# Batch 0's queries in token order by the copy out of PSUM, and corner zeros behind the next pair's copy: a blockwise-causal attention with a gated FFN on one core

## The chip, the cores and the metric

The kernel runs on one NeuronCore of one Trainium2 chip. The metric is the time of one execution on the device, in microseconds. The engines are named as in the profile: PE is the tensor engine's matmuls and PEld its weight loads, DVE the vector engine, ACT the scalar engine, POOL is GpSimd, and SP the engine that issues most of the DMAs. Each engine works through its own instructions in program order.

## The reference

Queries, keys and values are float32 of shape (8 batches, 8 heads, 576 tokens, 64). The attention is causal by blocks of 64 tokens: a query sees all keys of its own block and of the blocks before it. The attention's output, with the heads side by side, is 4608 rows of 512, and goes through a gated FFN of width 1536.

```python
scores = (1 / np.sqrt(D)) * np.matmul(q, k.transpose(0, 1, 3, 2))
mask = (pos[:, None] // 64) >= (pos[None, :] // 64)
scores = np.where(mask, scores, -1e9)
attn = softmax(scores)
x = np.matmul(attn, v).transpose(0, 2, 1, 3).reshape(4608, 512)
out = (np.maximum(x @ w_gate, 0.0) * (x @ w_val)) @ w_out
```

## The kernel before

**Tiles.** The first 512 tokens of a batch are four chunks of 128 (`c`), the last 64 are the tail. Heads go in pairs: a pair's two heads lie on partitions 0 to 63 and 64 to 127. A block of work `r` is a batch and a pair, `r = 4 * b + hp`. The tiles `qTm` and `kTm` hold a batch's queries and keys transposed, [128 partitions, 4, 4 pairs, 128]; there are two of each, used in turn by the batches.

**How queries and keys get there.** Batches 0 and 1 are loaded by `Early.load_qk` so that a partition holds four neighbouring tokens (token = 4 * p + j): that makes the DMA's pieces long. `cast_qk` makes bfloat16 of them. `pe_mains` (L351) then transposes a pair on PE, first four matmuls for the queries and then four for the keys, each into a bank of PSUM; the columns come out with `j` outermost. Two copies, `evac[0]` for the queries and `evac[1]` for the keys, take them to SBUF. The key copy (L365) reads PSUM with `j` inside, so `kTm` is in token order. For batch 0 alone, the query copy (L363) keeps `j` outermost, and `qTm` of batch 0 is [partition, j, pair, p].

**Scores.** `scores` (L464) makes scores transposed: keys are the stationary operand, queries the moving one, one matmul for each chunk of keys and each head of the pair. For chunk `c` it takes queries from chunk `c` on, so 512, 384, 256 or 128 columns. The function `queries` (L457) gives the moving operand. For batch 0 it puts the tokens in order in the read itself: for each `m`, the four `j` that are 512 elements apart. For the other batches the read goes along memory within a chunk.

```python
if b == 0:
    return m[ps, :, hp, 32 * c : 128].rearrange("p j m -> p m j")
return m[ps, c:4, hp, :]
```

`scores_of(g)` (L481, batch 0) does a third of a block: chunk 0, chunks 1 and 3, or chunk 2, into one of two pairs of score banks in turn, and ACT takes the exponential (L479) of both heads at once. `scores_all` does a whole block for the later batches. `corners` and `corner` (L536 to L544) zero the 64 x 64 corners of the diagonal chunks that the mask forbids, after the exponentials. `head_av` (L591) multiplies by the values (L605), with a column of ones that gives the sum; `normalise` (L549) divides by it; `to_xT_pe` (L645) transposes the result for the FFN.

**FFN.** `ffn_gen` (L684) is a generator: for a batch, 12 groups of gate and value matmuls (L700), ReLU on ACT (L709), the product on DVE (L714), then the output matmuls (L729). `ffn(n)` emits at least `n` matmuls of it; `ffn_parts(n)` emits `n` parts of four matmuls.

**Order.** All engines' orders are written out by hand (`manual_schedule`, from L788). Batch 0 comes first: for its four pairs, `pe_mains` with the copies on (DVE, ACT) for pair 0 and (DVE, DVE) for the other three, between calls of `scores_of` 0 to 11. Then value matmuls and transposes, with 12 FFN matmuls between them, and then the FFN of batch 0 in full. POOL does the casts of queries, keys, values and weights, and most of batch 0's corners. SP's queue loads, in order, batch 0's queries, keys and values, the FFN weights by halves, batch 1, and the tails. PSUM has eight banks; 6 and 7 (`AV`) are used by the value matmuls, by `pe_mains` of batch 1, and by `sort_v` (L300), which puts batch 1's values in token order by matmuls (L308).

Block 4 (the first of batch 1) is reached inside the FFN of batch 0. Its order is the second place that the change touches:

```python
e1.pe_mains(0, (dve, act), banks[:, AV : AV + 2])
ffn(8)
scores_all(4, False)
corners(4, nc.vector)
e1.pe_mains(1, (dve, act), banks[:, AV : AV + 2])
ffn(8)
e1.sort_v(0, (dve, act), banks[:, AV : AV + 2])
```

Of the kernel before, what the change touches and what calls it, by code (L numbers as in the profile page):

```python
# [17 lines left out]
def kernel(  # L18
# [29 lines left out]
    banks = psum.tile([128, 8, 512], FP, name="banks")  # L48
    AV = 6
# [8 lines left out]
    def pair():  # L58
        return take(2)

    def as_bf(bank):
        return bank.bitcast(BF)
# [8 lines left out]
    qTm = [consts.tile([128, 4, 4, 128], BF, name=f"qTm{i}") for i in range(2)]  # L71
    kTm = [consts.tile([128, 4, 4, 128], BF, name=f"kTm{i}") for i in range(2)]
    qTt = [consts.tile([128, 4, 64], BF, name=f"qTt{i}") for i in range(2)]
# [113 lines left out]
    class Early:  # L187
# [163 lines left out]
        def pe_mains(self, hp, evac, out=None):  # L351
            out = out or pair()
            for t in range(2):
                tp = as_bf(out[:, t, :])[:, 0:512]
                src = self.half(t, hp // 2)
                lo = 128 * (hp % 2)
                for j in range(4):
                    nc.tensor.transpose(  # L358
                        tp[:, 128 * j : 128 * j + 128], src[:, j, lo : lo + 128], ident
                    )  # L360
                dst = (qTm, kTm)[t][self.b % 2][:, :, hp, :]
                if self.b == 0 and t == 0:
                    evac[t](dst, tp.rearrange("p (j m) -> p j m", j=4))  # L363
                else:
                    evac[t](  # L365
                        dst.rearrange("p c (n j) -> p c n j", j=4),
                        tp.rearrange("p (j c n) -> p c n j", j=4, c=4),
                    )

        def pe_tails(self, evac):  # L370

# [82 lines left out]
            eng(dst, st)  # L454


    def queries(b, ps, c, hp):  # L457

        m = qTm[b % 2]
        if b == 0:  # L460
            return m[ps, :, hp, 32 * c : 128].rearrange("p j m -> p m j")
        return m[ps, c:4, hp, :]

    def scores(b, hp, sc, pieces):  # L464
        for pos, c, main in pieces:
            for hh in range(2):
                ps = slice(64 * hh, 64 * hh + 64)
                n = 512 - 128 * c if main else 64
                x = queries(b, ps, c, hp) if main else qTt[b % 2][ps, hp, :]
                o = sc[:, hh, pos : pos + n]  # L470
                if main:
                    o = o.rearrange("p (m n) -> p m n", n=4 if b == 0 else 128)
                nc.tensor.matmul(  # L473
                    o, kTm[b % 2][ps, c, hp, :], x, start=True, stop=True
                )
        return sc

    def exp(out, sc):
        nc.scalar.activation(out, sc, AF.Exp, scale=scale)  # L479

    def scores_of(g):  # L481

        r, i = divmod(g, 3)
        pieces = [[(0, 0, True)], [(0, 1, True), (384, 3, True)], [(0, 2, True)]][i]
        lo, hi = [(0, 512), (512, 1024), (1024, 1280)][i]
        sc = scores(0, r, banks[:, 0:2] if g % 2 == 0 else banks[:, 2:4], pieces)
        exp(attn(r, lo, hi), sc[:, :, 0 : hi - lo])

    def scores_all(r, tails=True):

        b, hp = divmod(r, 4)
        at = attnT[r % 2]
        sc = [
            scores(b, hp, pair(), [(0, 0, True)]),
            scores(b, hp, pair(), [(0, 1, True), (384, 3, True)]),
            scores(
                b, hp, pair(),
                [(0, 2, True)]
                + [(256 + 64 * c, c, False) for c in range(4 if tails else 0)],
            ),  # L500
        ]
        for hh in range(2):
            exp(at[:, hh, 0:512], sc[0][:, hh, :])
        exp(at[:, :, 512:1024], sc[1])
        w = 512 if tails else 256
        exp(at[:, :, 1024 : 1024 + w], sc[2][:, :, 0:w])
# [29 lines left out]
    def corners(r, eng):  # L536

        at = attnT[r % 2]
        three = at[64:128, :, 0:1536].rearrange("p g (c n) -> p g c n", c=3)
        eng.memset(three[:, :, :, 0:64], 0.0)  # L540
        eng.memset(at[64:128, :, 896:960], 0.0)
# [213 lines left out]
    def ffn(n):  # L755

        done[0] += n
        while part[0] < done[0]:
            ended = False
            while not ended:  # L760
                ended = next(gen, None)
                if ended is None:
                    return
                part[0] += 4
# [22 lines left out]
    dve, act, pool = nc.vector.tensor_copy, nc.scalar.copy, nc.gpsimd.tensor_copy  # L787
    with tc.manual_schedule(engines={E.PE, E.DVE, E.Activation, E.Pool, E.SP}):  # L788
# [64 lines left out]
        e1 = Early(1)  # L853
# [21 lines left out]
        e1.pe_mains(0, (dve, act), banks[:, AV : AV + 2])  # L875
        ffn(8)
        scores_all(4, False)
        corners(4, nc.vector)
        e1.pe_mains(1, (dve, act), banks[:, AV : AV + 2])
        ffn(8)  # L880
        e1.sort_v(0, (dve, act), banks[:, AV : AV + 2])
        ffn(8)
# [53 lines left out]
        for r in range(8, 4 * B):  # L936
            b, hp = divmod(r, 4)
# [78 lines left out]
```

## Time and profile before

| | |
|---|---|
| median of 3 runs | 378.8 us |
| lowest and highest run | 377.69 and 378.98 us |
| the profiled execution | 378.14 us |
| its span | 376.3 us |
| mean granted clock of the tensor engine | 0.982 |

The profile shows one execution. Times in it count from the start of the span. A group of instructions is a line, an engine, an operation and its tiles, with its count, its busy time, the mean of one in nanoseconds, and, behind the bar, the engine's idle time just ahead of them and what ended it. The chain of waits goes back from the last instruction, at each step to what released it. Tile names in batch 0's exponentials (`attnT`, `v_p`, `wo`) are buffers that lend their space.

### The profile page before, as it was taken

To read this page: it belongs to the slowest core of one execution; us is meant where nothing else is said; L and a number is where in the kernel's file an instruction comes from. 1 tells how busy PE (TensorE), PEld (TensorE's weight loads), DVE (VectorE), ACT (ScalarE), POOL (GpSimd) and SP (SyncE) were. 2 spreads that over 40 slices of the span, in tenths; PEclk is the share of its full clock that TensorE was granted. 3 is DMA by queue.
4 is the path that set the end of the run, shared out by engine and by line. 5 is a ranking of instruction groups with operands and counts; after the bars stand their busy time and mean duration, and the time that the engine had idled before them with its cause. 6 is when DMAs were issued, how large, how long until landed. Compare 5 with 4: busy or idle time off the path is not lost.

```text
span 376.3 us, 7510 instructions
## 1 busy us (share of the span) xinstructions
PE 367.1 (98%) x2993; PEld 189.5 (50%) x2993; DVE 164.7 (44%) x329; ACT 171.6 (46%) x269; POOL 116.0 (31%) x161
## 2 busy tenths in 40 slices
PE   7999989999999999999999999999999999999995
PEld 2354445555555555555555455545555554444443
DVE  4434345356655654354434443444344434323432
ACT  4644554755856654365436543654355503302310
POOL 5586764656908600950095005000000000000000
PEclk9669999999999999999999999999999999999999
DMA  8999999989999973996299639154301130020003
GB/s 251 292 371 358 371 210 308 169 206 253 158 108 134 128 136 66 133 166 131 62 154 152 109 85 141 42 102 92 99 17 17 44 101 1 3 84 28 2 34 106
DMA packets 139891, 51.02 MB, mean 136 GB/s; under 512 B 119504, under 2 KB 133072, under 8 KB 139856
## 3 DMA queue, kind: packets, MB, share of 16 engines
q1 hardware_dynamic: 78448, 34.29, 40.4%
q0 software_dynamic: 56704, 8.13, 37.1%
q10 hardware_dynamic: 4704, 8.13, 6.0%
q8 instruction: 23, 0.38, 0.4%
q14 instruction: 12, 0.10, 0.1%
HBM read 37.75 MB, written 9.44 MB: 125 GB/s over the span
## 4 chain that ended last, share of the span: by engine, by line
PE 96%; ACT 1%; DVE 1%; issue 0%; POOL 0%; DVEq 0%; ACTq 0%; POOLq 0%
PE banks L700 50%; PE banks L729 25%; PE banks L605 8%; PE banks L473 8%; PE banks L358 1%; PE banks L650 1%; PE banks L777 1%; PE banks L572 1%; PE banks L308 1%; ACT attnT L479 0%; DVE hT L714 0%; DVE ob L741 0%; ACT v_p L479 0%; ACT kTt L384 0%; PE banks L512 0%
## 5 line engine op out<-in xcount | busy, mean ns | idle before, releaser
L479 ACT ACTIVATE attnT<-banks 128x1024 bf16<-128x1024 f32 (+1 forms) x118 | 85.1, 805 | 63.4 <-PE banks L473 63.4
L709 ACT ACTIVATE gate_sb<-banks 128x512 bf16<-128x512 f32 x108 | 65.0, 603 | 101.4 <-PE banks L700 101.1
L714 DVE TENSOR_TENSOR hT<-gate_sb,banks 128x512 bf16<-128x512 bf16 x108 | 74.0, 688 | 78.8 <-PE banks L700 75.0
L700 PE MATMUL banks<-xT,wg 128*128 128x512 bf16 x384 | 99.8, 382 | 1.2 <-DVE xT L655 0.8
L700 PE MATMUL banks<-xT,wv 128*128 128x512 bf16 x384 | 98.5, 379 | 0.0
L729 PE MATMUL banks<-wo,hT 128*128 128x512 bf16 (+1 forms) x444 | 97.0, 373 | 0.0
L700 PEld LDWEIGHTS <-wv 128*128 128x128 bf16 x432 | 42.3, 98 | 51.0
L729 PEld LDWEIGHTS <-hT 128*128 128x128 bf16 x444 | 42.4, 98 | 46.1
L700 PEld LDWEIGHTS <-wg 128*128 128x128 bf16 x432 | 40.6, 98 | 46.2 <-issue 2.3
L741 DVE COPY ob<-banks 128x512 f32<-128x512 f32 (+1 forms) x37 | 25.1, 677 | 56.0 <-PE banks L729 55.9
L408 POOL DMA_DIRECT2D v_bf<-in_v_dram x16 | 14.3, 910 | 78.9 <-PE banks L605 78.9
L605 PEld LDWEIGHTS <-attnT 128*128 128x128 bf16 x792 | 29.9, 99 | 11.1 <-issue 3.3
L605 PE MATMUL banks<-v_bf,attnT 128*128 128x65 bf16 x792 | 34.5, 196 | 0.0
L473 PE MATMUL banks<-qTm,kTm 64*128 64x512 bf16 (+3 forms) x256 | 31.6, 349 | 1.3 <-DVE hT L714 0.4
L554 DVE TENSOR_TENSOR xnat<-banks,recip 128x640 bf16<-128x640 f32 (+2 forms) x36 | 25.9, 721 | 1.4 <-DVE recip L553 0.2
L553 DVE RECIPROCAL recip<-banks 128x10 f32<-128x10 f32 (+3 forms) x38 | 8.0, 210 | 35.7 <-PE banks L605 34.1
L473 PEld LDWEIGHTS <-kTm 64*128 64x128 bf16 x512 | 16.5, 95 | 12.3 <-issue 3.1
L540 DVE MEMSET attnT<- 64x192 uint32 x28 | 6.1, 218 | 22.0 <-ACT attnT L479 19.1
L408 POOL DMA_DIRECT2D k_bf<-in_k_dram x16 | 14.1, 911 | 1.4 <-DMA v_bf<-in_v_dram 1.4
L408 POOL DMA_DIRECT2D q_bf<-in_q_dram x16 | 14.3, 937 | 0.5 <-DMA v_bf<-in_v_dram 0.5
L700 PE MATMUL banks<-xTt,wg 128*128 128x512 bf16 x48 | 12.3, 379 | 0.0
L700 PE MATMUL banks<-xTt,wv 128*128 128x512 bf16 x48 | 12.3, 379 | 0.0
(101 smaller groups left out, 207.7 us busy)
## 6 DMA issues: line engine op xcount, KB each, us to landing
out_dram<-ob ACTq DMA_DIRECT2D x28, 256.0 KB, 2.2
stage<-in_moe_w_gate_dram SPq DMA_DIRECT2D x6, 512.0 KB, 9.3
stage<-in_moe_w_val_dram SPq DMA_DIRECT2D x6, 512.0 KB, 9.4
stage<-in_q_dram SPq DMA_DIRECT2D x6, 512.0 KB, 6.4
stage<-in_k_dram SPq DMA_DIRECT2D x6, 512.0 KB, 7.6
stage<-in_moe_w_out_dram SPq DMA_DIRECT2D x6, 512.0 KB, 9.7
stage<-in_v_dram SPq DMA_DIRECT2D x8, 256.0 KB, 6.3
q_bf<-in_q_dram POOLq DMA_DIRECT2D x16, 128.0 KB, 6.0
```

The costliest lines, as they stand in the source:

```text
L408: nc.gpsimd.dma_start(dst, src[b, :, 128 * c : 128 * c + n, :].rearrange("h p d -> p h d"),)
L473: nc.tensor.matmul(o, kTm[b % 2][ps, c, hp, :], x, start=True, stop=True)
L479: nc.scalar.activation(out, sc, AF.Exp, scale=scale)
L540: eng.memset(three[:, :, :, 0:64], 0.0)
L553: nc.vector.reciprocal(recip, av[:, :, :, 64])
L554: nc.vector.tensor_tensor(out=out, in0=av[:, :, :, 0:64], in1=recip.to_broadcast([rows, heads, n, 64]), op=AX.mult,)
L605: nc.tensor.matmul(av[:, 0, p, :], w, vb[:, c, h, :], start=(p == 0), stop=(c == p), skip_group_check=True,)
L700: nc.tensor.matmul(out[f][:, t, :], (wg, wv)[t][i][:, c, fo : fo + 128], x[:, c, :], start=(c == 0), stop=(c == 3),)
L709: nc.scalar.activation(gate[f], out[f][:, 0, :], AF.Relu)
L714: nc.vector.tensor_tensor(out=h, in0=gate[f], in1=out[f][:, 1, :], op=AX.mult)
L729: nc.tensor.matmul(ops[:, g, 0 : n1 - n0], hT[f][:, 128 * s : 128 * (s + 1)], wo[i][:, f % 4, n0:n1], start=(f == 0), stop=(f == 11),)
L741: nc.vector.tensor_copy(ob, ops[:, g, 0 : n1 - n0])
```

## The change

The query copy of batch 0 takes the form of the key copy: it reads PSUM with `j` inside and writes `qTm` along memory in token order. The function `queries` goes; the scores of batch 0 read their moving operand as those of the other batches do, and the view of the output follows. The number of matmuls, copies and columns is the same.

Besides, `corners(4)` on DVE is put behind `e1.pe_mains(1)`, whose query copy is on DVE too. The two swap places in DVE's order; no other engine's order changes.

```diff
@@ -358,14 +358,12 @@ (pe_mains)
-                dst = (qTm, kTm)[t][self.b % 2][:, :, hp, :]
-                if self.b == 0 and t == 0:
-                    evac[t](dst, tp.rearrange("p (j m) -> p j m", j=4))
-                else:
-                    evac[t](
-                        dst.rearrange("p c (n j) -> p c n j", j=4),
-                        tp.rearrange("p (j c n) -> p c n j", j=4, c=4),
-                    )
+                evac[t](
+                    (qTm, kTm)[t][self.b % 2][:, :, hp, :].rearrange(
+                        "p c (n j) -> p c n j", j=4
+                    ),
+                    tp.rearrange("p (j c n) -> p c n j", j=4, c=4),
+                )
@@ -454,22 +452,15 @@
-    def queries(b, ps, c, hp):
-
-        m = qTm[b % 2]
-        if b == 0:
-            return m[ps, :, hp, 32 * c : 128].rearrange("p j m -> p m j")
-        return m[ps, c:4, hp, :]
-
     def scores(b, hp, sc, pieces):
...
-                x = queries(b, ps, c, hp) if main else qTt[b % 2][ps, hp, :]
+                x = qTm[b % 2][ps, c:4, hp, :] if main else qTt[b % 2][ps, hp, :]
                 o = sc[:, hh, pos : pos + n]
                 if main:
-                    o = o.rearrange("p (m n) -> p m n", n=4 if b == 0 else 128)
+                    o = o.rearrange("p (c n) -> p c n", n=128)
@@ -875,8 +866,8 @@
         scores_all(4, False)
+        e1.pe_mains(1, (dve, act), banks[:, AV : AV + 2])
         corners(4, nc.vector)
-        e1.pe_mains(1, (dve, act), banks[:, AV : AV + 2])
         ffn(8)
```

## The prediction

> **What bounds the kernel now.** I read the page first, then the chain of waits over the first 60 us, then the groups by form around the changed lines, the clock by windows, and last the timeline at the two edits. The first fence is a line of the page: the tensor engine (PE) is busy for nearly the whole span, so the question is where its busy time is not work at its full rate. In the chain (start, length, what) every piece that carries the batch 0 score matmuls (L473) is shown, and the first FFN pieces.
>
> ```profile
> PE 367.1 (98%) x2993; PEld 189.5 (50%) x2993; DVE 164.7 (44%) x329; ACT 171.6 (46%) x269; POOL 116.0 (31%) x161
> ```
>
> ```profile
> 6.57 1.89 PE banks L473 x6
> ...
> 9.91 1.02 PE banks L473 x2
> ...
> 11.48 1.39 PE banks L473 x6
> ...
> 13.84 0.96 PE banks L473 x2
> ...
> 15.46 0.96 PE banks L473 x3
> ...
> 17.09 0.53 PE banks L473 x2
> ...
> 18.28 0.95 PE banks L473
> ...
> 19.90 0.96 PE banks L473 x2
> ...
> 21.40 0.52 PE banks L473
> ...
> 23.56 1.71 PE banks L700 x4
> ...
> 29.29 13.11 PE banks L700 x60
> ```
>
> The nine L473 pieces add up to 9.18 us of the first 22 us. From 29.29 on the chain is FFN matmuls (L700) with hardly a break, so a microsecond won ahead of 29.29 moves all that follows, as long as its inputs are there.
>
> Why these pieces are long shows in the groups by form. The first four rows are batch 0 (window 5.6 to 22.6), where the moving operand is read with j inside, a jump for every element; the two after them are batch 1 (window 50 to 54), where it is read along memory. Mean ns of one is behind the comma.
>
> ```profile
> L473 PE MATMUL banks<-qTm,kTm 64*128 64x512 bf16 x8 | 4.1, 1020 | 0.6 <-DVE kTm L365 0.4 <-ACT kTm L365 0.2
> ...
> L473 PE MATMUL banks<-qTm,kTm 64*128 64x384 bf16 x8 | 3.2, 810 | 0.0
> ...
> L473 PE MATMUL banks<-qTm,kTm 64*128 64x256 bf16 x8 | 2.4, 594 | 0.0
> L473 PE MATMUL banks<-qTm,kTm 64*128 64x128 bf16 x8 | 1.6, 392 | 0.0
> ```
>
> ```profile
> L473 PE MATMUL banks<-qTm,kTm 64*128 64x512 bf16 x2 | 0.4, 386 | 0.0
> ...
> L473 PE MATMUL banks<-qTm,kTm 64*128 64x128 bf16 x2 | 0.2, 216 | 0.0
> ```
>
> Strided, 384 more columns cost 1020 - 392 = 628 ns, 1.64 ns each; along memory 386 - 216 = 170 ns, 0.44 ns each. The two heads of a pair run side by side (two matmuls of 1.02 us are one piece of 1.02 at 9.91), so a form counts once. The windows (length, then PE, PEld, DVE, ACT, POOL busy, then the granted clock, DMA share, GB/s) show the clock in the same stretch:
>
> ```profile
> 9.05:12.46 3.41, 3.04 (x18) 0.78 (x16) 1.82 (x4) 2.14 (x3) 2.53 (x6) 1.00 1.37 220
> 12.46:15.87 3.41, 3.41 (x24) 1.57 (x24) 1.45 (x4) 2.54 (x3) 1.85 (x5) 0.50 1.14 308
> 15.87:19.28 3.41, 3.41 (x31) 1.47 (x28) 1.49 (x5) 1.62 (x3) 1.35 (x6) 0.50 1.10 350
> 19.28:22.70 3.42, 3.42 (x36) 1.88 (x36) 1.11 (x4) 2.64 (x3) 3.42 (x4) 0.50 1.06 386
> 22.70:26.11 3.41, 3.41 (x31) 2.28 (x29) 1.38 (x8) 0.96 (x2) 2.68 (x4) 0.50 1.06 371
> 26.11:29.52 3.41, 2.62 (x27) 1.44 (x25) 1.41 (x5) 0.58 (x2) 2.53 (x3) 1.00 1.10 349
> ```
>
> The clock is 0.50 from 12.46 to 26.11, although PE is shown busy without a gap. The strided 512-column piece is as long inside that stretch (0.96 at 18.28) as before it (1.02 at 9.91): it is bound by its reads, not by the clock. Work along memory does follow the clock: the four 512-column FFN matmuls at 23.56 took 1.71, so 0.43 each at half clock.
>
> **Part 1, the scores of batch 0.** Removed: the strided read. There are 4 x (512 + 384 + 256 + 128) = 5120 columns. I put the first 1792 (through the piece at 9.91) at full clock, 0.44 ns each, 0.8 us, and the other 3328 at half clock, 0.43 us per 512, 2.8 us: 3.6 us in place of 9.18, 5.6 us less for PE alone.
>
> But the exponentials on ACT then bound this stage. The five groups of batch 0's exponentials, and the first and last in the timeline (start, length):
>
> ```profile
> L479 ACT ACTIVATE attnT<-banks 128x1024 bf16<-128x1024 f32 x4 | 4.0, 1022 | 2.4 <-PE banks L473 2.4
> L479 ACT ACTIVATE v_p<-banks 128x1024 bf16<-128x1024 f32 x2 | 2.0, 1024 | 1.5 <-PE banks L473 1.5
> L479 ACT ACTIVATE wo<-banks 128x1024 bf16<-128x1024 f32 x2 | 2.0, 1023 | 1.6 <-PE banks L473 1.6
> L479 ACT ACTIVATE wo<-banks 128x512 bf16<-128x512 f32 x2 | 1.2, 597 | 0.2 <-PE banks L473 0.2
> L479 ACT ACTIVATE attnT<-banks 128x512 bf16<-128x512 f32 x2 | 1.2, 594 | 0.0
> ```
>
> ```profile
> 7.63 2.54 ACT L479 ACTIVATE attnT<-banks 128x1024 bf16<-128x1024 f32 x3 [1.12 <-PE banks L473]
> ...
> 8.83 0.42 DVE L363 COPY qTm<-banks 128x512 bf16<-128x512 bf16 x1 [2.80 <-PE banks L358]
> ...
> 9.17 0.68 DVE L365 COPY kTm<-banks 128x512 bf16<-128x512 bf16 x1
> ...
> 20.90 1.67 ACT L479 ACTIVATE wo<-banks 128x1024 bf16<-128x1024 f32 x2 [0.60 <-PE banks L473]
> ```
>
> Eight large and four small ones are 8 x 1.02 + 4 x 0.60 = 10.6 us. The first can start 0.43 after the first score, at 7.0 (0.386 plus the 0.04 seen now between 7.59 and 7.63), so the last ends no sooner than 17.6; now it ends at 22.57. The gain at that point is at most 5.0 us. Below, if every handover between PE, ACT and the two pairs of score banks costs what ACT waits now after such a change of pair (about half of the 5.7 us of idle in the groups stays), it is some 2.8. I take 4.5, near the ACT bound, because PE needs less time per head pair (0.6 us of scores at full clock for 1280 columns, 1.1 at half) than the 2.65 us that its three exponentials take, with the transposes and value matmuls besides: the last exponential ends near 18.1.
>
> Added: the query copy takes the form of the key copy, on DVE 0.68 instead of 0.42 (the rows at 9.17 and 8.83), 0.26 more four times. For the first pair DVE copies queries while ACT copies keys, and ACT ends later: nothing. For the other three the keys' copy is queued behind the queries' on DVE, and the scores of that pair behind the keys. This is covered because the transposes that release the copies come earlier too: pair 1's follow the first two score blocks, which end about 1.3 us sooner, so its keys are there about 1.1 us sooner than 9.85, near 8.8, while the score banks are held by the second exponential until about 9.0. If that cover is gone it costs 3 x 0.26 = 0.8 us, and the lower end holds that.
>
> **Part 2, from the last exponential to 29.29.** This stretch (last value matmuls, transposes, the first 12 FFN matmuls) lasts 29.29 - 22.57 = 6.7 us, 3.5 of them at half clock. About 1.2 us of it no clock shortens: 0.8 in which PE is idle in the last window (busy 2.62 of 3.41), waiting for the last transposed copies, and some 0.4, an estimate, in which the last transposes' results are on their way; PE's own work is then about 1.8 at full rate ahead of 26.11 and 2.0 behind it, 3.8. Starting at 18.1, the clock decides. The unbroken run of short matmuls and FFN now begins shortly ahead of the window 22.70 to 26.11, and the clock is back at that window's end. Begun 4 us sooner, it fills the window 19.28 to 22.70, so I let the clock return at 22.70: 4.6 us at half clock do 2.3 of the 3.8, 1.5 remain, and 1.2 of copies: 18.1 + 4.6 + 1.5 + 1.2 = 25.4. The gain at the FFN's start is 29.29 - 25.4 = 3.9 us.
>
> The Trainium skill, "TensorE: Matmul & The Clock Gate", Part 1, says that the array runs at half rate unless a window of about 3.4 us was busy, and the granted clock here changes after 13.65 us, four windows of 3.41, which agrees. It gives no measure of busy that would explain why 15.87 to 22.70 did not count here, with PE shown busy throughout.
>
> Are the inputs there? The last cast of the second weight block, and the FFN step that needs it:
>
> ```profile
> 26.89 1.04 POOL L454 CAST wv<-stage 128x1024 bf16<-128x1024 f32 x1 [0.34 <-DMA stage<-in_moe_w_val_dram]
> ...
> 34.47 1.03 PE L700 MATMUL banks<-xT,wv 128*128 128x512 bf16 x4
> ```
>
> The cast waits for its DMA and will not come sooner; it ends at 27.93, 6.5 us ahead of its use. A gain of under 6.5 us passes.
>
> **Part 3, the corner zeros.** The memsets of block 4 wait for that block's exponentials, and the query copy is queued behind them on DVE.
>
> ```profile
> 47.34 0.62 ACT L365 COPY kTm<-banks 128x512 bf16<-128x512 bf16 x1
> 47.65 0.22 DVE L540 MEMSET attnT<- 64x192 uint32 x1 [2.28 <-ACT attnT L479]
> ...
> 47.97 0.69 DVE L365 COPY qTm<-banks 128x512 bf16<-128x512 bf16 x1
> ...
> 48.72 1.05 PE L308 MATMUL banks<-v_p,sel 64*128 64x256 bf16 x16 [0.75 <-DVE qTm L365]
> ```
>
> DVE idles 2.28 us ahead of the memset. Moved, the query copy runs in that hole. The value sort (L308), which reuses the copy's banks, then waits for the key copy on ACT, 47.34 + 0.62 = 47.96, not for 48.66: 0.70 of PE's 0.75 us go. What is late next is that ACT copy, which stays behind the exponentials. The memsets start when they do now; the multiply queued behind them waits for its gate on ACT in any case, and the value matmuls that read the zeros come behind two more FFN blocks and the next pair's scores. No DMA or other queue is passed.
>
> **The sum.** 3.9 + 0.7 = 4.6 us. The profiled execution took 378.14 (span 376.3 and 1.8 around it): 373.5. The median of the runs shown is 378.8, 0.7 above it; I forecast 374.0, between 373.5 and 378.8 - 4.6 = 374.2. A change of about 0.5% (1.9 us) is what can be told from none.
>
> **The rivals.**
> - The clock comes back no earlier. For: it is one observation, and a window may miss by a little. Work from 18.1 at half clock to 26.11 would be 4.0 at full rate, just over the 3.8: the FFN starts at about 26.6, the gain is 2.7 + 0.7, time 374.7; one window later still, another 3.41 / 2 = 1.7 us goes: 376.4. Against: less waiting in the same windows. 23%.
> - The clock comes back earlier, at 19.28, since the contiguous scores are denser work: 1.2 us at half do 0.6, 3.2 remain, 1.2 of copies: 23.7, gain 5.6 + 0.7, time 371.8. Against: 15.87 to 19.28 still has waits for ACT. 8%.
> - The wait only moves: key copies, zeros on POOL and value casts take the place of the strided reads, and the lower end of part 1, less 0.8 of late key copies, is what is left: 2.0 at the last exponential, of which part 2 gives back about 0.9 at half clock, and 0.7 from part 3: 1.8 us, 376.3, or 377.0 from the median. For: POOL works in order and is busy 2.5 of 3.41 in the window from 9.05. Against: all of ACT's idle time in these groups is put down to L473. 10%.
> - Slower: the strided matmuls are what keeps the gate from a longer cold stretch. With short scores PE stands idle while ACT works, and the half-clock stretch doubles, from 13.65 us to 27.3, until about 39.8. Against the first rival (gain 3.4) this loses 13.65 / 2 = 6.8 us of dense FFN: 378.14 - 3.4 + 6.8 = 381.5. It decides for slower when more than about 11 us of FFN beyond 26.11 run at half clock. Against: 22.70 to 26.11, with the same kind of dense work, brought the clock back. The same page of the Trainium skill, in "HAM oscillation", tells of clocks that fall again at idle gaps of over 3.4 us; no such gap is in this trace after 29.29. 5%.
>
> **How the numbers follow.** The forecast has 54%, with its own range 372.5 to 375.3 from part 1 between 3.0 and 5.0. The range 371.8 to 376.7 takes in the clock rivals and leaves out the slower one, most of the moved wait and tails. Faster by over 0.5% (below 376.9): the forecast, both clock rivals and some of the moved wait, 87%; within: most of the moved wait and part of the clock's cost, 8%; slower 5%.
>
> **What would show it.** Batch 0's 512-column score form should read about 0.39 us at full clock and about 0.6 at half; the DVE query copies of batch 0 0.68; ACT's idle time ahead of the exponentials should fall from 5.7 us to about 1; the last of them should end at 17.6 to 18.5, the unbroken FFN run begin near 25.4, and the clock be 1.00 from about 22.7. The wait of L308 should fall from 0.75 to under 0.1 and name ACT. The forecast is wrong if the score form stays near 1 us, if the FFN start moves by under 2 us, or if waits for weights or inputs come up after it.

## The result, and the profile after

| | before | after |
|---|---|---|
| median of 6 runs each | 378.78 us | 374.12 us |
| lowest and highest | 377.69, 378.98 | 373.69, 376.35 |
| the profiled execution | 378.14 | 376.35 |
| its span | 376.3 | 374.6 |
| its mean granted clock | 0.982 | 0.991 |

The ratio after to before is 0.9898, 95% interval 0.9873 to 0.9923. By the ratio, for which two more runs of the changed kernel (375.71 and 374.62 us) count too, the gain is 3.9 us (2.9 to 4.8). The profiled execution of the changed kernel is the slowest of its six; part of the reason for the spread is at the end of this section.

Line numbers are smaller by up to 9: the scores are L464, the exponentials L470, the FFN L691, both copies L361, the output copies L732, the stores of batch 0's FFN L667. First the groups by form, window 5.6 to 22.6, which answer to those of before:

```profile
L470 ACT ACTIVATE attnT<-banks 128x1024 bf16<-128x1024 f32 x4 | 3.9, 1021 | 0.6 <-PE banks L464 0.6
L361 DVE COPY qTm<-banks 128x512 bf16<-128x512 bf16 x4 | 2.8, 691 | 3.4 <-PE banks L358 3.3
...
L470 ACT ACTIVATE v_p<-banks 128x1024 bf16<-128x1024 f32 x2 | 2.0, 1023 | 0.0
L470 ACT ACTIVATE wo<-banks 128x1024 bf16<-128x1024 f32 x2 | 1.9, 1020 | 0.0
...
L464 PE MATMUL banks<-qTm,kTm 64*128 64x512 bf16 x8 | 1.6, 383 | 0.8 <-ACT attnT L470 0.6
...
L464 PE MATMUL banks<-qTm,kTm 64*128 64x128 bf16 x8 | 0.9, 216 | 0.0
```

The 512-column score form went from 1020 to 383 ns, the query copy from 425 to 691. ACT hardly waits for scores (0.6 us in all, 5.7 before), and scores now wait for ACT: the exponentials bound the stage. The windows, with the granted clock behind the five busy times:

```profile
9.05:12.46 3.41, 2.75 (x35) 1.85 (x36) 2.38 (x4) 3.41 (x6) 2.48 (x6) 1.00 1.37 218
12.46:15.87 3.41, 3.28 (x57) 2.12 (x53) 2.87 (x10) 3.41 (x5) 2.65 (x10) 1.00 1.13 314
15.87:19.28 3.41, 3.23 (x56) 2.25 (x55) 2.20 (x12) 2.17 (x4) 2.63 (x3) 1.00 1.09 350
19.28:22.70 3.42, 2.64 (x16) 1.26 (x15) 0.82 (x4) 0.77 (x2) 1.68 (x3) 1.00 1.05 385
22.70:26.11 3.41, 3.41 (x17) 1.57 (x16) 1.97 (x3) 1.85 (x4) 2.79 (x3) 1.00 1.06 370
```

The clock does not fall: 1.00 where it was 0.50 from 12.46 to 26.11. In the timeline, the first and the last exponentials of batch 0, the start of the unbroken FFN run, and the value sort:

```profile
7.22 4.85 ACT L470 ACTIVATE attnT<-banks 128x1024 bf16<-128x1024 f32 x6 [0.60 <-PE banks L464]
...
13.96 3.01 ACT L470 ACTIVATE wo<-banks 128x512 bf16<-128x512 f32 x4
...
21.89 0.59 PE L691 MATMUL banks<-xT,wg 128*128 128x512 bf16 x2 [0.78 <-DVE xT L646]
...
40.70 1.14 PE L308 MATMUL banks<-v_p,sel 64*128 64x256 bf16 x16
```

The last exponential ends at 16.97 (22.57 before), the FFN run starts at 21.89 (29.29), the sort, which no longer waits, at 40.70 (48.72). At these three places the changed kernel is 5.6, 7.4 and then 8.0 us ahead of the kernel before. Yet the span is only 1.7 us shorter. The rest is given back at one place:

```profile
50.22 0.69 DVE L732 COPY ob<-banks 128x512 f32<-128x512 f32 x1 [2.22 <-PE banks L720]
...
55.88 0.41 POOL L180 CAST v_bf<-stage 64x256 bf16<-64x256 f32 x1 [0.65 <-DMA stage<-in_v_dram]
...
57.78 0.86 POOL L180 CAST v_bf<-stage 64x256 bf16<-64x256 f32 x2
...
58.59 1.80 POOL L667 DMA_DIRECT2D out_dram<-ob  x3
...
64.59 0.69 DVE L732 COPY ob<-banks 128x512 f32<-128x512 f32 x1 [6.15 <-DMA out_dram<-ob]
65.33 0.37 PE L464 MATMUL banks<-qTm,kTm 64*128 64x256 bf16 x1 [4.71 <-DVE ob L732]
```

The first output copy is done at 50.9, but its store is issued on POOL's queue, behind the casts of batch 1's tails (`Tails.cast`). Those wait in part for their loads (the row at 55.88) and end at 58.6. There are three output buffers (`ob`), so the fourth copy waits until the first store has landed, 64.5. DVE stands still for 6.15 us, PE for 4.71. And behind that the clock falls, as the windows show:

```profile
60.90:64.80 3.90, 0.00 (x0) 0.00 (x0) 0.21 (x1) 1.43 (x3) 3.52 (x4) 1.00 1.19 311
64.80:68.20 3.40, 2.87 (x35) 2.10 (x35) 1.57 (x4) 0.98 (x2) 0.00 (x0) 0.51 1.09 212
68.20:71.70 3.50, 3.50 (x66) 3.05 (x65) 0.78 (x4) 3.22 (x6) 1.40 (x3) 0.50 0.62 119
71.70:75.10 3.40, 3.40 (x37) 2.03 (x36) 1.13 (x3) 0.18 (x1) 1.00 (x1) 1.00 0.97 187
```

That costs another 1.6 us: the lead of 8.0 is 3.4 behind the wait and 1.8 from 71.7 to the end. In the runs near the median the mean clock was 0.994 or 0.995, and in those over 375 us 0.991: that fits a half-clock stretch of one window of 3.4 us or of two.

### The profile page after: what moved, and what is told of

It reads as the page before. It is cut to its first block, busy times and chain, and to the rows that moved or that the text cites. A ratio compares the mean times of both kernels' runs of the same rounds, so it can differ in the third digit from the quotient of the medians.

```text
span 374.6 us, 7510 instructions
## 1 busy us (share of the span) xinstructions
PE 360.9 (96%) x2993; PEld 189.5 (51%) x2993; DVE 163.6 (44%) x329; ACT 171.2 (46%) x269; POOL 116.7 (31%) x161
## 4 chain that ended last, share of the span: by engine, by line
PE 82%; DMA 13%; SPq 3%; POOL 1%; issue 0%; DVE 0%; POOLq 0%; DVEq 0%
PE banks L691 44%; PE banks L720 22%; PE banks L596 7%; PE banks L464 6%; DMA stage<-in_moe_w_out_dram 3%; DMA stage<-in_moe_w_gate_dram 3%; DMA stage<-in_moe_w_val_dram 3%; DMA stage<-in_v_dram 2%; DMA out_dram<-ob 2%; SPq L223 1%; SPq L170 1%; DMA stage<-in_k_dram 1%; PE banks L563 1%; PE banks L381 0%; PE banks L641 0%
## 5 line engine op out<-in xcount | busy, mean ns | idle before, releaser
L470 ACT ACTIVATE attnT<-banks 128x1024 bf16<-128x1024 f32 (+1 forms) x118 | 85.0, 805 | 65.0 <-PE banks L464 65.0
L691 PE MATMUL banks<-xT,wg 128*128 128x512 bf16 x384 | 99.1, 380 | 1.0 <-DVE xT L646 0.8
L691 PE MATMUL banks<-xT,wv 128*128 128x512 bf16 x384 | 98.7, 379 | 0.0
L691 PEld LDWEIGHTS <-wv 128*128 128x128 bf16 x432 | 42.2, 98 | 51.3 <-POOL wv L452 0.5
L691 PEld LDWEIGHTS <-wg 128*128 128x128 bf16 x432 | 40.5, 98 | 46.0 <-issue 1.8
L732 DVE COPY ob<-banks 128x512 f32<-128x512 f32 (+1 forms) x37 | 25.0, 677 | 60.6 <-PE banks L720 54.3
L464 PE MATMUL banks<-qTm,kTm 64*128 64x512 bf16 (+3 forms) x256 | 25.5, 299 | 6.7 <-DVE ob L732 4.7
L464 PEld LDWEIGHTS <-kTm 64*128 64x128 bf16 x512 | 17.2, 96 | 11.7 <-issue 2.1
L691 PE MATMUL banks<-xTt,wg 128*128 128x512 bf16 x48 | 12.3, 379 | 0.0
L691 PE MATMUL banks<-xTt,wv 128*128 128x512 bf16 x48 | 12.3, 379 | 0.0
```

The lines of the kernel that those rows point to most:

```text
L464: nc.tensor.matmul(o, kTm[b % 2][ps, c, hp, :], x, start=True, stop=True)
L691: nc.tensor.matmul(out[f][:, t, :], (wg, wv)[t][i][:, c, fo : fo + 128], x[:, c, :], start=(c == 0), stop=(c == 3),)
L732: nc.vector.tensor_copy(ob, ops[:, g, 0 : n1 - n0])
```

## The experiments

My theory then: the read's gain, some of it through the clock, is about 7.4 us where batch 0's FFN starts, and a store queued on POOL takes back what exceeds its slack (A). The rivals are named in the expectations. Each ratio below is to the kernel before on the same chip.

**e1, the query change alone.**

```diff
         scores_all(4, False)
-        e1.pe_mains(1, (dve, act), banks[:, AV : AV + 2])
         corners(4, nc.vector)
+        e1.pe_mains(1, (dve, act), banks[:, AV : AV + 2])
```

> The changed kernel with corners(4) back in its old place. In the changed kernel's profile PE is 8.0 us ahead of the kernel before at the value sort, then waits 4.7 us for the fourth output copy, which waits for a buffer whose store POOL issues only behind the tail casts (58.59). Theory A (that store sets a fixed time, and whatever was won ahead of it beyond some 3.4 us is lost there): L308 waits 0.7 us again, the wait for the output copy is about 4.0 instead of 4.7, and the time is that of the changed kernel, 374.1, within 0.3 us. Rival B (the 0.7 us of the corner edit adds to the end): 374.8 to 374.9.

Measured: 374.71 us, ratio 0.9915 (0.9893 to 0.9936), which overlaps that of the full change; the time lies 0.6 us above theory A's and just under rival B's. Timeline, and the window in which the clock is at half:

```profile
41.87 1.05 PE L308 MATMUL banks<-v_p,sel 64*128 64x256 bf16 x16 [0.75 <-DVE qTm L361]
...
64.26 0.27 PE L464 MATMUL banks<-qTm,kTm 64*128 64x256 bf16 x1 [2.56 <-DVE ob L732]
```

```profile
66.00:69.40 3.40, 3.40 (x66) 3.00 (x66) 0.99 (x6) 3.27 (x6) 0.07 (x1) 0.50 0.62 116
```

L308's wait is back, and PE's wait for the output copy is 2.56, not 4.0: the store was issued at 58.12 and landed at 63.5, a microsecond sooner than in the other profile. So the time of landing differs between two profiles by more than the 0.7 us in question, and whether the corner edit adds to the end in the changed kernel is not settled by this run.

**e2, the corner edit alone**, made in the kernel before (the diff is the last hunk of the change).

> The kernel before with the corner edit alone. Both theories: the wait of L308 falls from 0.75 to under 0.1 us. Theory A: ahead of the store's time there is room for this (the store was issued at 59.15, 0.6 us behind the tail casts' earliest end, and its buffer used long after), so it reaches the end: 378.8 - 0.7 = 378.1. Rival B: the same 378.1. If something behind L308 takes it up, 378.8.

Measured: 377.35 us against 378.02, ratio 0.9986 (0.9977 to 0.9996): 0.5 us by the ratio (0.2 to 0.9), 0.7 by the medians. Between runs with the same mean clock it is 0.7 as well: about 377.3 against 378.0 at 0.980 to 0.982, and 378.0 against 378.9 at 0.976 or 0.977. At L308 PE waits for nothing any more:

```profile
46.57 0.69 DVE L365 COPY qTm<-banks 128x512 bf16<-128x512 bf16 x1 [0.69 <-PE banks L358]
47.85 0.62 ACT L365 COPY kTm<-banks 128x512 bf16<-128x512 bf16 x1
48.16 0.22 DVE L540 MEMSET attnT<- 64x192 uint32 x1 [0.90 <-ACT attnT L479]
48.41 1.14 PE L308 MATMUL banks<-v_p,sel 64*128 64x256 bf16 x16
```

The query copy runs ahead of the zeros and is done at 47.26. The prediction had ACT's key copy as the next to be waited for (47.85 + 0.62 = 48.47); PE shows no wait for it.

**e3, the full change, with batch 0's output stores on ACT's queue.**

```diff
-            (nc.gpsimd if j == 0 else nc.scalar).dma_start(out[r0 : r0 + 128, :], ob)
+            nc.scalar.dma_start(out[r0 : r0 + 128, :], ob)
```

> The changed kernel with the four output stores of batch 0's FFN issued from ACT's queue, as all others are, instead of POOL's. Theory A (the stores wait on POOL behind the tail casts, and a clock that falls after 4 us of idle PE adds to it): the fourth output copy no longer waits, PE's 4.7 us and the half-clock stretch from 64.9 to 71.7 go; PE stays 7.5 to 8 us ahead: 370.3 to 371.3. Rival C (stores are slow because the DMA engines are full with the loads, wherever they are issued; or batch 2's inputs are late next): at least half of the wait stays in the same place or a little behind, 372.5 to 374.1.

Measured: 371.44 us, ratio 0.9822 (0.9809 to 0.9836), clear of the full change's interval, and just above theory A's 370.3 to 371.3. In the timeline, and then in what was asked of the tile `ob`:

```profile
51.17 0.36 ACTq L667 DMA_DIRECT2D out_dram<-ob  x1
...
60.24 0.69 DVE L732 COPY ob<-banks 128x512 f32<-128x512 f32 x1 [1.58 <-PE banks L720]
```

```profile
DMA to landing us min/median/max: 3.7/5.9/6.1
```

The same answer for the full change, with POOL's queue:

```profile
DMA to landing us min/median/max: 5.8/5.9/6.0
```

From either queue a store takes a median of 5.9 us to land, so slow stores are not the cause; the first is issued 7.4 us sooner (51.17, not 58.59). The fourth copy waits for its matmuls alone, the half-clock stretch is gone (mean clock 1.000), and PE keeps its lead to the end: the span of this profile, taken from the fastest of the five runs, is 368.7, 7.6 under that of before. This version is faster than both kernels.

**e4, the same stores on ACT's queue in the kernel before** (a control).

> Control: the kernel before with the same four stores on ACT's queue. Theory A: nobody waits for those stores in the kernel before, so the time stays within 0.3 us of 378.8. If the store's queue is worth something by itself, it is faster than that by over 0.5 us, and the gain of e3 is not that of a wait that the change brought up.

Measured: 378.19 us against 378.02, ratio 1.0008 (0.9999 to 1.0016). Nobody waited for those stores there, so what e3 wins over the change is a wait that the change itself brought up.

**e5, the copy's cost without the read's gain**: e3, with the strided read of the kernel before.

```diff
-                x = qTm[b % 2][ps, c:4, hp, :] if main else qTt[b % 2][ps, hp, :]
+                x = qTt[b % 2][ps, hp, :]
+                if main and b == 0:
+                    x = qTm[0][ps, :, hp, 32 * c : 128].rearrange("p j m -> p m j")
+                elif main:
+                    x = qTm[b % 2][ps, c:4, hp, :]
...
-                    o = o.rearrange("p (c n) -> p c n", n=128)
+                    o = o.rearrange("p (m n) -> p m n", n=4 if b == 0 else 128)
```

> The kernel of e3 (change and stores on ACT), with the query copy in token order as in the change, but batch 0's score matmuls reading with the old jump of 512 elements, so their scores are not the reference's: the copy's cost without the read's gain. Theory A (it is the read that cost the time, and the clock falls because matmuls that wait for their operand do not count as work for the clock gate): the 512-column form is back near 1.02 us, the clock falls to half near 12.5 for four windows, the unbroken FFN run starts near 29.3 to 30, L308 waits under 0.1, time 377.3 to 378.2. Rival D (the clock is luck of the window's phase, or comes from the order of the copies): the clock stays at 1.00 and the FFN starts 2 to 4 us sooner than that, about 374 to 376.

Measured: 378.16 us, ratio 0.9996 (0.9983 to 1.0008). Group, windows and timeline:

```profile
L468 PE MATMUL banks<-qTm,kTm 64*128 64x512 bf16 x8 | 4.1, 1021 | 0.6 <-ACT attnT L474 0.6
```

```profile
7.22:10.64 3.42, 2.78 (x18) 0.76 (x14) 1.29 (x2) 2.54 (x3) 2.31 (x5) 1.00 1.26 271
10.64:27.70 17.06, 17.06 (x137) 8.81 (x136) 7.24 (x23) 9.00 (x11) 12.15 (x20) 0.50 1.11 339
```

```profile
30.56 0.59 PE L695 MATMUL banks<-xT,wg 128*128 128x512 bf16 x2 [0.79 <-DVE xT L650]
```

Without the contiguous read nothing of the gain is left, and the clock and the FFN's start are back where they were; rival D is out. The clock fell sooner than I had expected (10.64) and stayed at half for five windows instead of four, and the FFN starts at 30.56, 0.6 us behind what I expected at the latest. What the longer query copies cost here shows in ACT's idle time ahead of pair 1's first exponential, in e5 and then in e2, which has the old copies and as long a half-clock stretch:

```profile
11.56 1.02 ACT L474 ACTIVATE attnT<-banks 128x1024 bf16<-128x1024 f32 x1 [1.06 <-PE banks L468]
...
11.07 1.02 ACT L479 ACTIVATE attnT<-banks 128x1024 bf16<-128x1024 f32 x1 [0.80 <-PE banks L473]
```

That is 0.26 us, one copy. Ahead of the first exponential the two differ by 0.1 us, and ahead of all later ones by 0.01 at most. So even with the strided read only one copy lies on the path, not the three (0.8 us) that the prediction put in its lower end.

**e6, the read's gain without the copy's cost**: e3, with the query copy of the kernel before.

> The kernel of e3 with the query copy of the kernel before (0.42 us, j outermost), and the scores reading along memory: the queries of batch 0 are not in token order, so the mask falls on the wrong ones. It is the read's gain without the copy's cost. Theory A: the copy is covered by the exponentials, so at most 0.3 us are won: 371.1 to 371.5. Rival E (the keys' copy, late by 0.26 us for three pairs, is on the path): 0.8 us, 370.6.

Measured: 372.28 us, ratio 0.9862 (0.9806 to 0.9919), not under e3 and above theory A's range; of the four runs one took 376.33, with a mean clock of 0.990; the cause of that is open. The FFN's start:

```profile
21.80 0.59 PE L693 MATMUL banks<-xT,wg 128*128 128x512 bf16 x2 [0.79 <-DVE xT L648]
```

It is at 21.89 in the full change and at 22.31 in e3. So the cheaper copy wins 0.1 to 0.5 us there at most, no more than the two kernels with the same copy differ by (0.4); the 0.8 of rival E is not there.

**e8, no warming matmuls**: e3, without the `junk` matmuls.

```diff
-        junk(7, banks[:, 0])
...
-        junk(2, banks[:, 7])
```

> The kernel of e3 without the nine warming matmuls of zeros ahead of and behind the first transposes. It puts the contiguous scores at half clock, to price the clock apart from the read. Theory A: the granted clock is 0.50 over most of the attention of batch 0 and comes back at the end of a window densely filled with value matmuls and FFN, as forecast near 22.7; PE is then 3.5 to 4.5 us ahead of the kernel before at the FFN's start instead of 7.0, and the time 374 to 375. Rival F (the clock matters little here, since ACT bounds the stage): ahead by over 6 us still, 371.4 to 372.2.

Measured: 371.85 us, ratio 0.9836 (0.9815 to 0.9856). The 512-column score form, up to 15.2 and behind 15.3, and the FFN's start:

```profile
L464 PE MATMUL banks<-qTm,kTm 64*128 64x512 bf16 x6 | 1.8, 604 | 1.3 <-ACT kTm L361 0.7 <-DVE kTm L361 0.6
...
L464 PE MATMUL banks<-qTm,kTm 64*128 64x512 bf16 x2 | 0.4, 386 | 0.0
```

```profile
23.55 0.59 PE L691 MATMUL banks<-xT,wg 128*128 128x512 bf16 x2 [0.79 <-DVE xT L646]
```

The trace has no record of the clock ahead of 15.24, where it is recorded as full, but the same form takes 604 ns ahead of it and 386 behind it: the matmuls ahead ran at half. My theory failed here. The time is rival F's, and the lead at the FFN's start, 5.7 us, is just under the 6 that it named: with contiguous reads a start at half clock costs only 1.2 us there (23.55 against 22.31). ACT waits 2.2 us for scores in all, 1.0 in e3, so it bounds most of the stage still, and the clock comes back inside the attention, not in the FFN.

**e9 and e10, the strided read in two of the four pairs** (e5 with `and hp < 2` or `and hp > 1`), one run each. The strided read is the same in amount, and only its place differs.

> The kernel of e3 with the old strided read in the scores of pairs 0 and 1 alone (their scores are not the reference's; pairs 2 and 3 read along memory). Theory G (the clock falls because matmuls that wait for their operand leave the array idle in the windows from 5.6 to 12.5): the clock falls to half at 9 to 13 as in all kernels with the strided read in all four pairs, and is back sooner than their 26 to 28, near 16 to 20, because the work behind it is dense; the FFN's unbroken run starts near 24 to 25. Rival H (what counts is the stretch from 12.5 on, or the total): no fall of the clock, and only the 2 x 2.2 us of longer reads less what ACT covers, FFN near 24.

> The same with the strided read in pairs 2 and 3 alone. Theory G: the windows to 12.5 are as in e3, so the clock does not fall there; PE has value matmuls between the strided ones from then on, and either does not fall at all or falls one window later, near 15 to 16, and returns by 22 to 24: FFN's unbroken run at 24 to 26. Rival H: the clock falls as in the kernels with all four pairs strided, at 9 to 13.

```profile
7.16:10.57 3.41, 2.77 (x18) 0.76 (x14) 1.29 (x2) 2.54 (x3) 2.45 (x5) 1.00 1.16 277
10.57:17.40 6.83, 6.83 (x52) 3.29 (x50) 3.37 (x7) 4.43 (x5) 4.08 (x10) 0.50 0.97 274
17.40:20.80 3.40, 3.35 (x60) 2.34 (x59) 2.76 (x9) 3.27 (x6) 2.77 (x6) 1.00 1.11 369
```

```profile
7.04:13.87 6.83, 5.54 (x56) 2.77 (x52) 4.47 (x8) 5.87 (x7) 5.30 (x11) 1.00 1.26 262
13.87:24.11 10.24, 10.24 (x97) 5.92 (x94) 3.82 (x16) 5.43 (x7) 6.69 (x11) 0.50 1.08 367
24.11:27.50 3.39, 2.60 (x22) 1.35 (x20) 1.29 (x5) 0.37 (x1) 2.75 (x3) 1.00 1.09 356
```

The first three rows are e9, the others e10. The fall follows the strided matmuls: at 10.57 where the first two pairs are strided, with the return at 17.40; at 13.87 where it is the last two, with the return at 24.11. The last exponential and the start of the FFN run, e9 first:

```profile
17.52 3.16 ACT L474 ACTIVATE wo<-banks 128x512 bf16<-128x512 f32 x4
...
25.60 0.59 PE L695 MATMUL banks<-xT,wg 128*128 128x512 bf16 x2 [0.79 <-DVE xT L650]
```

```profile
18.61 1.66 ACT L474 ACTIVATE wo<-banks 128x1024 bf16<-128x1024 f32 x2 [0.61 <-PE banks L468]
...
27.12 0.59 PE L695 MATMUL banks<-xT,wg 128*128 128x512 bf16 x2 [0.79 <-DVE xT L650]
```

This prices the clock apart from the read. From the end of the last exponential to the FFN run it is 4.92 us in e9, where the clock is back by then, and 6.85 in e10, where it is at half for 3.84 us of that stretch; half of that is the difference of 1.93. The other profiles agree: 4.92 or 4.93 in the full change, e3, e6 and e8, all at full clock there, and 6.72 in the kernel before, with 3.54 us at half (22.57 to 26.11).

The times were 373.83 and 375.34 us against 378.07. Theory G held in kind: the clock fell in e9, and in e10 it fell behind 13 us, both against rival H. Its sizes were short, with FFN starts 0.6 and 1.1 us later than expected at the latest, and e10's fall came 1.1 us sooner than expected. Why the clock falls in these windows, in which PE is shown busy, was not measured by itself: that matmuls which wait for their operand do not count as work fits the profiles, and no run tests it apart from the strided read.

## Why the prediction was right, and where its steps failed

The time was forecast as 374.0 and measured as 374.12, but that is luck: two errors of over 3 us cancel in it. The FFN run began 3.5 us sooner than forecast (21.89, not 25.4), and the output stores, which the prediction did not look at, gave back about as much. Of the signs that it named, the last exponential, the FFN's start and the clock did not come as stated, and a wait for weights came up, which it had named as a sign of being wrong.

- **The read and the copies** came as stated: 383 ns for the 512-column form (0.39 forecast; at half clock 604 in e8, 0.6 forecast), 691 for the copy (0.68), ACT's idle time near 1 (0.6). The copies' cover held in the changed kernel (e6); the price without it, 0.8 us, was too high (0.26 in e5).
- **Part 1 was mis-sized.** I took 4.5 us at the last exponential and held 5.0 for the most; it is 5.6. The bound added up twelve means end to end. The row at 7.22 shows six in 4.85 us where their means give 4 x 1.02 + 2 x 0.60 = 5.3: neighbours overlap by about 0.1 in the profile.
- **Part 2 failed on the clock.** I let it fall as before and return at 22.70, which gave back 0.6 us of part 1. It did not fall, so the 3.5 us that were at half clock before became 1.8 shorter (6.72 to 4.92 from the last exponential to the FFN run; e9 and e10 differ by 1.9): 5.6 + 1.8 = 7.4 in place of 3.9. The rows were there: two windows with PE shown busy throughout and the clock still at half. I wrote that no measure of busy explained them, and did not ask whether the change removes the cause. The rival of an earlier clock was nearest, and was short too (23.7).
- **Part 3 was right by itself**: 0.7 forecast, 0.5 to 0.7 measured (e2). What it adds at the end of the changed kernel is open (e1).
- **The inputs** had the slack stated, 6.5 us, and the lead went over it. PE's weight load waited for the cast of the second weight block, and its four matmuls took 1.23 us instead of 1.03:

```profile
27.68 0.11 PEld L691 LDWEIGHTS <-wv 128*128 128x128 bf16 x2 [0.52 <-POOL wv L452]
```

- **The stores were not looked at.** I asked only whether inputs were there, and counted the queues that the moved instruction passes. An earlier start also moves what leaves. Two rows of before show how little slack it had:

```profile
59.15 0.71 POOL L676 DMA_DIRECT2D out_dram<-ob  x1 [1.00 <-DVE ob L741]
...
67.94 0.69 DVE L741 COPY ob<-banks 128x512 f32<-128x512 f32 x1 [1.58 <-PE banks L729]
```

POOL had idled 1.00 us ahead of the store, so with the casts ahead of it where they are the store can come at most 1.0 us sooner, however early its data is. The fourth copy, at 67.94, is 3.4 us behind the landing of the store in the profile after, 64.5: of 8.0 us of lead 3.4 are left, as seen. The moved-wait rival had the right kind and the wrong place (keys, zeros and values of batch 0).

So the sum in the profiled execution is 5.6 + 1.8 + 0.6 - 4.6 - 1.6 = 1.8 us: the last exponential, the FFN's start and the sort, less the store and the half clock behind it. The medians differ by 4.7, where 4.6 was forecast from 3.9 + 0.7. No trace of a run at the median was kept, so how the 4.7 divides is not shown; nearest is e1's profile, at 374.17 us, with a wait of 2.56 us and one half-clock window. Of the slower rival one part was seen, half clock behind a stretch in which PE stands idle; it came from the store's wait, and lasted 3.4 to 6.8 us instead of 13.65 more.

## What to carry to other kernels

A moving operand read with a jump for every element can be paid twice on TensorE, as here: in its own length (1.02 us in place of 0.38), and in the clock of the work behind it (1.8 us up to the FFN run). Put the permutation into a copy that other work covers. When a stage will come earlier, list what its outputs need as well as its inputs: each store's queue, what is queued ahead of it there, and how many buffers stand between it and the next writer. A forecast whose number comes out right should still be checked at the milestones in between: here the FFN's start was off by 3.5 us.

## What the runs showed of the hardware

- The strided 512-column read took 1.02 us at full and at half clock; along memory it took 0.38 at full and 0.60 at half (e8).
- All profiles with the strided read in four pairs had the clock at half for four or five windows, 13.65 or 17.06 us, while the profile shows PE busy for 98% of it or more (17.06 of 17.06 in e5); with two strided pairs it was 6.83 or 10.24 us, and in the contiguous ones that began warm the clock did not fall in that stage. Why it is four windows in one run and five in another was not found.
- Exponentials that follow each other on ACT overlap in the profile by about 0.1 us, so a sum of their durations is no lower bound for the stage: twelve that add up to 10.6 us took 9.75.
- The Trainium skill, "TensorE: Matmul & The Clock Gate", "HAM oscillation", puts the fall of the clock at idle gaps of over about 3.4 us. The 4.71 us gap agrees, but in e1 a gap of 2.56 us was followed by a half-clock stretch of 3.4 us too, and 0.50 stood for 17 us where the profile shows no gap at all; here the measurements decide.
